# A decay attention and two gated layers on one core: the first layer in two halves for two chunks, fp32 scores on alternating row halves, clustered attention matmuls, early two-operand work on VectorE

## The chip, the cores and the metric

The kernel runs on one core of a Trainium2 chip. The metric is the device time of one execution in microseconds (us). Three runs of the kernel before gave 1046.68, 1047.19 and 1048.68; the median is 1047.19.

The engines in the text: TensorE (PE in the rows; PEld is its weight load), VectorE (DVE), ScalarE (ACT), GpSimd (POOL) and SyncE (SP), which issues the DMA transfers. Each runs its own instructions in the order in which they were issued.

## What is computed

Three stages, each the input of the next. B, H, S, D are 4, 8, 768, 48; the token matrix has 3072 rows of 384.

```python
for t in range(S):                       # attention with a decaying state
    cur = np.einsum('bhd,bhe->bhde', u[None] * kt, vt)
    y[:, :, t] = np.einsum('bhd,bhde->bhe', rt, state + cur)
    state = wt[:, :, :, None] * state + np.einsum('bhd,bhe->bhde', kt, vt)
x = y as (B * S, H * D)
xn = x / np.sqrt(np.mean(x * x, -1) + 1e-6) * rms_g
x = (silu(xn @ w_gate) * (xn @ w_val)) @ w_out     # 384 -> 1536 -> 384, the "first MoE"
g = s * np.maximum(x @ w_in, 0.0) ** 2 + b         # 384 -> 2048, the "second MoE"
out = g @ w_out2                                   # 2048 -> 384
```

The weights come in as 64-bit floats. The result has to be more exact than one matmul of 12-bit parts, so each MoE product is three matmuls: high times high, high times low, low times high.

## The kernel before, in words

**Tiling.** The sequence is cut into six chunks of 128 steps. One chunk of all four batch rows is 512 tokens, the widest matmul. A *pair* (number `jb` = 4 x chunk + batch row, 24 of them) is one batch row's chunk, all eight heads.

**Attention of a pair** (`attention`, L277). VectorE scans the decays forward (L296) and backward (L303); r and k are multiplied with the two results (L257); GpSimd forms the state decay (L309). TensorE makes the scores of four heads that lie on partitions 0 to 47 and of four on 64 to 111 (L332), transposes k (L347), adds up the state's part (L359) and the scores times v (L365), and forms the state's update (L382). ScalarE copies the scores out of PSUM, GpSimd masks them (L337). Then VectorE adds the current step's part, GpSimd computes the row scale (L391, L393), and `attention_x` (L477) transposes the result (L484) into `XH` and `XL`, the high and low parts (L492). From pair 8 on (`FINE = 8`) the scores are made in a finer way: `split_scores` (L423) splits k and r in high and low parts (ScalarE L428 to L432, VectorE or GpSimd L434, L437), multiplies those (L448), adds the pieces, masks them (L455), and splits the masked scores in three bf16 parts (L460, L462); the sums are then six bf16 products (L370).

**First MoE.** A step is one `f` of twelve (128 of the 1536 inner columns): gate and value products (L560), SwiGLU on ScalarE and VectorE, a split of the result in high (`hh`) and low (`hl`) parts, and three output products (L545 to L547) that add up in PSUM banks 2 to 4 over the twelve steps. Per step that is 27 matmuls. At a chunk's end `store` copies the banks out and SP writes them to a scratch tensor `x2d`. Chunk 0 does its first four steps in two token halves of 256 (`HALF = 4`).

**Weights** (`weights`, L497). For each `f` SP loads two blocks of 64-bit words; VectorE builds the 32-bit pattern in three passes (L524, L528, L530) of 768 and of 384 elements, ScalarE takes the high part (L534), VectorE or GpSimd the low part (L536, three per `f`). All 36 tiles of the first MoE stay in SBUF; during chunk 5 the second MoE's tiles overwrite them.

**Second MoE.** Per chunk `x2_in` loads the stored result, splits it, and 16 steps of 18 matmuls follow. Beside them VectorE checks the range of all decays and weights (L656, L673 to L681).

**Order.** Nothing is ordered by hand. Every operation is given to a planner (`Plan`, L96) with a due time, a cost per engine that can do it, and what it reads and writes. It runs through the list in its own time; when an engine comes free, the ready operation with the least due time goes next, and that order is issued. Where an operation names VectorE and GpSimd, the planner picks the one that is free. The due times come from the constants at L44 and the sums over chunks (`dur`, `beg`).

Of the kernel before, what the change touches and what calls it, by code (L numbers as in the profile page):

```python
# [33 lines left out]
G = 16  # L34
# [61 lines left out]
class Plan:  # L96
    """Operations with the engines that can run them, what they read and what they write.

    Each engine runs its operations in the order in which they are issued, so they are issued
    in the order in which they come to be ready: of those that are ready when an engine comes  # L100
    free, the one with the least `when` goes first."""

    PASS = 0.2
# [5 lines left out]
    def add(self, when, engines, fn, reads=(), writes=()):  # L109
# [8 lines left out]
        self.ops.append((when, engines, fn))  # L118
        self.deps.append(deps)

    def issue(self):
# [7 lines left out]
        free = dict.fromkeys(ready, 0.0)  # L129
        done = [False] * n  # L130
# [3 lines left out]
        while events:  # L134
# [8 lines left out]
            for e, queue in ready.items():  # L143
                while queue and free[e] <= now:
# [5 lines left out]
                    cost, late = self.ops[i][1][e]  # L150
                    free[e] = now + cost
                    heapq.heappush(events, (free[e], 0, i))
                    for k in users[i]:
                        left[k] -= 1
                        start = max(now + cost + late, getattr(self, "t%d" % k, 0.0))
                        setattr(self, "t%d" % k, start)
                        if not left[k]:
                            heapq.heappush(events, (start, -1, k))
# [13 lines left out]
def act(n):  # L172
    return 0.20 + 0.55e-3 * n


def gps(n):
    return 0.15 + 2.1e-3 * n


def mm(n, k=1):  # L180
    return k * (0.003 + n / 2400.0)
# [3 lines left out]
def body(ctx: ExitStack, tc: tile.TileContext, rkw, nat, w1, w2, cst, out):  # L185
# [15 lines left out]
    RAW, PAT, SKR, SA = [None] * 2, [None] * 2, [None] * 2, [None] * 2  # L201
# [27 lines left out]
    x2d = [dr.tile([KD, 128, NB], F32, name=f"x2d{c}") for c in range(NC)]  # L229
# [25 lines left out]
    def tt(when, engines, n, dst, a, b, f, reads, writes):  # L255
        cost = {"dve": vec2(n), "pool": gps(n)}
        op(when, {e: cost[e] for e in engines}, lambda e: E[e].tensor_tensor(dst, a, b, f), reads, writes)  # L257
# [19 lines left out]
    def attention(jb, t, quick):  # L277
        q, b = jb % 2, jb % B
        ke, re, ne = QUICK[jb] if quick else (POOL if jb < 2 * B else BOTH, BOTH, BOTH)
# [12 lines left out]
        else:  # L292
# [3 lines left out]
        op(t, {"dve": vec2(HP * WL)}, lambda e: nc.vector.tensor_tensor_scan(  # L296
            ET.rearrange("p h t -> p (h t)"), a[:, 0:HP * WL], ones.rearrange("p h t -> p (h t)"), 0.0,
            ALU.mult, ALU.add), [("w", q), "c"], ["E"])
        op(t, {"pool": 0.06}, lambda e: nc.gpsimd.memset(
            a[:, 0:HP * WL].rearrange("p (h t) -> p h t", h=HP)[:, :, G + 1:C:G], 0.0), ["E"], [("w", q)])  # L300
        op(t, {"dve": 0.27}, lambda e: nc.vector.reciprocal(
            g.rearrange("p (h t) -> p h t", h=HP)[:, :, G - 1:C:G], ET[:, :, G:WL:G]), ["E"], [("g", q)])
        op(t, {"dve": vec2(HP * WL)}, lambda e: nc.vector.tensor_tensor_scan(  # L303
# [4 lines left out]
        if not last:  # L308
            op(t, {"pool": 0.16}, lambda e: nc.gpsimd.tensor_tensor(  # L309
# [8 lines left out]
            AC[q].rearrange("p h o -> p (h o)"), n[0], AX.X, ALU.add), nk, [("ac", q)])  # L318
        tt(td, BOTH, DM, AV[q], v, AC[q].to_broadcast([128, H, D]), ALU.mult, [("ac", q), ("v", q)], [("av", q)])

        A = []
        fine = jb >= FINE
        if fine:
            A = split_scores(t, q, r, k)
            split_v(td, v, n, q)
        for p in range(0 if fine else 2):
            i, s = bank(jb), ring("a", (0, 1, 2))
            sc = PS[i].rearrange("p (h t) -> p h t", h=HP)

            def scores(e, p=p, sc=sc):  # L330
                for h in range(HP):
                    nc.tensor.matmul(sc[:, h, :], k[64 * p:64 * p + D, h, :], r[64 * p:64 * p + D, h, :],  # L332
                                     start=True, stop=True)

            op(t, {"pe": 0.88}, scores, [("k", q), ("r", q)], [("ps", i)])
            cp(t, HP * C, AT[s], sc, [("ps", i)], [("a", s)])
            op(t, {"pool": 0.59}, lambda e, s=s: nc.gpsimd.affine_select(  # L337
                out=AT[s], in_=AT[s], compare_op=ALU.is_gt, fill=0.0, base=0, pattern=[[0, HP], [1, C]],
                channel_multiplier=-1), (), [("a", s)])
            A.append(s)  # L340
        if not last:
# [3 lines left out]
            def turn_k(e, kp=kp):  # L345
# [569 lines left out]
```

## Time and profile before

| | us |
|---|---|
| median of three runs | 1047.19 |
| profiled execution, first to last instruction | 1042.2 |
| TensorE busy | 996.5 (96%) |
| VectorE busy | 745.1 (71%) |
| ScalarE busy | 466.5 (45%) |
| GpSimd busy | 387.8 (37%) |

The profile is of one execution; its own device time is not listed, so its span stands beside the median of the runs, 5.0 us below it. Matmul ends are modelled, so the length of a run of matmuls is read from start to next start. In the page's second part each digit is the busy share of a fortieth of the span (26.06 us) in tenths, and PEclk is the granted clock of TensorE in tenths of 2.4 GHz.

### The profile page before, as it was taken

The numbers are of one execution on the slowest core, as the hardware profiler recorded it, in microseconds if no ns is written. First come the engines' busy times: TensorE is split into PE (matmuls) and PEld (weight loads), VectorE is DVE, ScalarE is ACT, GpSimd is POOL, SyncE is SP. The second block draws the span as 40 slices with busy tenths as digits, with TensorE's granted clock in tenths as the row PEclk, the third lists the DMA queues.
The fourth block names the chain that finished last, engine by engine and source line by source line (L and its number), as shares of the span: only waits on it lengthen the run. The fifth ranks groups of instructions, "written<-read, shape, count | busy, mean of one in ns | idle before, by whom it ended". The sixth has DMA issues, their size and how long they took to land. (4 is left out here: it accounts for less than half of the span.)

```text
span 1042.2 us, 14486 instructions
## 1 busy us (share of the span) xinstructions
PE 996.5 (96%) x5438; PEld 828.6 (80%) x5438; DVE 745.1 (71%) x1115; ACT 466.5 (45%) x899; POOL 387.8 (37%) x389
## 2 busy tenths in 40 slices
PE   8787889999999999999999998999999999999997
PEld 7777778788888888888887776888888888888886
DVE  7999997776776787778669999999973343433333
ACT  2343436655656566665543334334343343433332
POOL 4898556555566556765534553000000000000000
PEclk6598989999999999999999999999999999999999
DMA  8445541212222121112257645757530000000001
GB/s 248 147 157 156 186 144 41 87 50 61 72 66 65 50 90 50 50 49 71 73 145 244 197 157 203 240 199 274 210 112 11 0 31 1 31 1 1 31 1 34
DMA packets 44046, 105.16 MB, mean 101 GB/s; under 512 B 3904, under 2 KB 18752, under 8 KB 43968
## 3 DMA queue, kind: packets, MB, share of 16 engines
q1 hardware_dynamic: 43968, 104.16, 31.1%
q8 instruction: 44, 0.72, 0.3%
q14 instruction: 34, 0.28, 0.1%
HBM read 94.70 MB, written 9.44 MB: 100 GB/s over the span
## 5 line engine op out<-in xcount | busy, mean ns | idle before, releaser
L560 PE MATMUL b<-xh,w 128*128 128x512 f32 (+1 forms) x1494 | 489.8, 389 | 6.6 <-DVE sg L257 2.4
L560 PEld LDWEIGHTS b<-xh,w 128*128 128x128 f32 x1494 | 282.1, 191 | 63.2 <-DVE sg L257 4.1
L560 PE MATMUL b<-xl,w 128*128 128x512 f32 (+1 forms) x747 | 288.2, 386 | 0.0
L546 PE MATMUL b<-hl,w 128*128 128x512 f32 (+1 forms) x519 | 201.8, 389 | 8.2 <-POOL hl L257 7.8
L545 PE MATMUL b<-hh,w 128*128 128x512 f32 (+1 forms) x519 | 205.5, 396 | 2.3 <-ACT hh L260 2.3
L547 PE MATMUL b<-hh,w 128*128 128x512 f32 (+1 forms) x519 | 200.4, 386 | 0.0
L260 ACT ACTIVATE sg<-b 128x512 f32<-128x512 f32 (+1 forms) x173 | 100.7, 582 | 184.4 <-PE b L560 181.1
L560 PEld LDWEIGHTS b<-xl,w 128*128 128x128 f32 x747 | 142.7, 191 | 25.8 <-DVE xl L492 0.2
L626 DVE SCALAR_TENSOR_TENSOR sg<-sg,cs,b 128x512 f32<-128x512 f32 (+1 forms) x97 | 71.8, 741 | 109.4 <-ACT sg L260 109.3
L546 PEld LDWEIGHTS b<-hl,w 128*128 128x128 f32 x519 | 98.4, 190 | 30.3 <-POOL hl L257 11.8
L545 PEld LDWEIGHTS b<-hh,w 128*128 128x128 f32 x519 | 98.4, 190 | 20.3 <-ACT hh L260 2.9
L547 PEld LDWEIGHTS b<-hh,w 128*128 128x128 f32 x519 | 98.2, 189 | 19.1
L629 DVE SCALAR_TENSOR_TENSOR hl<-sg,cs,hh 128x512 fp32r<-128x512 f32 (+1 forms) x97 | 72.2, 744 | 51.1 <-ACT hh L260 51.1
L260 ACT ACTIVATE hh<-sg,cs 128x512 fp32r<-128x512 f32 (+1 forms) x97 | 69.8, 720 | 82.1 <-DVE sg L626 75.6
L257 POOL TENSOR_TENSOR hl<-sg,hh 128x512 fp32r<-128x512 f32 (+1 forms) x52 | 76.7, 1474 | 72.8 <-ACT hh L260 69.1
L260 ACT ACTIVATE hh<-sg 128x512 fp32r<-128x512 f32 (+1 forms) x76 | 46.0, 605 | 67.3 <-DVE sg L257 66.6
L257 DVE TENSOR_TENSOR sg<-b,sg 128x512 f32<-128x512 f32 (+1 forms) x76 | 49.6, 652 | 27.9 <-PE b L560 27.7
L534 ACT ACTIVATE w<-pat 128x384 fp32r<-128x384 f32 x68 | 33.0, 517 | 72.6 <-DVE pat L530 69.5
L536 POOL TENSOR_TENSOR w<-pat,w 128x384 fp32r<-128x384 f32 x36 | 49.9, 1396 | 38.0 <-ACT w L534 38.0
L260 ACT ACTIVATE a<-b 128x256 f32<-128x256 f32 (+1 forms) x80 | 31.7, 417 | 37.4 <-PE b L448 21.4
L460 ACT ACTIVATE sa<-a 128x512 bf16<-128x512 f32 x64 | 39.2, 629 | 20.0 <-DVE a L462 17.3
L530 DVE SCALAR_TENSOR_TENSOR pat<-raw,pat 128x768 uint32<-128x768 uint32 (+1 forms) x40 | 44.0, 1101 | 0.2
(104 smaller groups left out, 1297.1 us busy)
## 6 DMA issues: line engine op xcount, KB each, us to landing
raw<-in_w SPq DMA_DIRECT2D x56, 768.0 KB, 4.6
in<-in_rkw SPq DMA_DIRECT2D x24, 448.0 KB, 3.7
raw<-in_w SPq DMA_DIRECT2D x24, 384.0 KB, 3.4
n<-in_nat SPq DMA_DIRECT2D x23, 384.0 KB, 3.1
in<-in_rkw SPq DMA_DIRECT2D x24, 226.6 KB, 2.5
a<-in_rkw SPq DMA_DIRECT2D x24, 224.0 KB, 3.3
v<-in_nat SPq DMA_DIRECT2D x24, 192.0 KB, 2.6
x2d<-o SPq DMA_DIRECT2D x18, 256.0 KB, 2.3
```

Source lines behind the costliest of these rows:

```text
L257: op(when, {e: cost[e] for e in engines}, lambda e: E[e].tensor_tensor(dst, a, b, f), reads, writes)
L260: op(when, {"act": act(n)}, lambda e: nc.scalar.activation(dst, src, func, **kw), reads, writes)
L460: op(t, {"act": act(N)}, lambda e, s=s, x=x, p=p: nc.scalar.activation(SA[p][:, x], AT[s], AF.Copy), [("a", s)], [("sa", p, x)])
L530: op(t, {"dve": vec2(N)}, lambda e, word=word, pat=pat: nc.vector.scalar_tensor_tensor(pat(), word(0), 29, pat(), ALU.logical_shift_right, ...
L534: op(t, {"act": act(DM)}, lambda e, c=c, s=s, pat=pat: nc.scalar.activation(W[s][:, 0], pat(c).bitcast(F32), AF.Copy), [("pat", pi)], [("w ...
L536: op(t, {"dve": vec2(DM), "pool": gps(DM)}, lambda e, c=c, s=s, pat=pat: E[e].tensor_tensor(W[s][:, 1], pat(c).bitcast(F32), W[s][:, 0].bi ...
L545: nc.tensor.matmul(dst, wt[:, 0, cols], xh, start=first, stop=False, skip_group_check=True)
L546: nc.tensor.matmul(dst, wt[:, 0, cols], xl, start=False, stop=False, skip_group_check=True)
L547: nc.tensor.matmul(dst, wt[:, 1, cols], xh, start=False, stop=last, skip_group_check=True)
L560: nc.tensor.matmul(dst, W[s][:, w, kk * 128:(kk + 1) * 128], xx[x][:, kk, sl], start=first and j == kk == 0, stop=last and kk == KD - 1 an ...
L626: op(t, {"dve": vec2(n)}, lambda e: nc.vector.scalar_tensor_tensor(sg, sg, s_col, p, ALU.mult, ALU.mult), [("ps", i)], [("sg", q)])
L629: op(t, {"dve": vec2(n)}, lambda e: nc.vector.scalar_tensor_tensor(hl, sg, b_col, hh.bitcast(F32), ALU.add, ALU.subtract), [("sg", q), ("h ...
```

## The change

1. **Two halves.** The first MoE's order was: all 12 steps for chunk 0, then for chunk 1, and so on. Now it is steps 0 to 5 for chunk 0, steps 0 to 5 for chunk 1, steps 6 to 11 for chunk 0, steps 6 to 11 for chunk 1, then all 12 for each later chunk. The first half's output sums of the two chunks go to scratch tensors of their own, and `x2_in` loads both and adds them. Chunk 1 does its first six steps in token halves too.
2. **fp32 scores for all pairs, alternating.** The split scores are gone. All pairs multiply k and r directly in fp32, and the matmuls of the two partition halves alternate, into two PSUM banks. The three-part bf16 sums remain, from pair 12 on (`FINE, EARLY = 12, 12`).
3. **Three clusters.** Scores of both halves and the transposes of k are one planner operation; sums of both halves and the state's update are another; the transposes of the result are the third.
4. **Early two-operand work on VectorE.** For pairs 2 to 11 the products of r, k and the current step's part name VectorE alone, as do the low parts of the first MoE's weights and of the SwiGLU result.
5. **The planner.** Costs are changed, the delay from one engine to the next is a number per engine, and two-operand work of VectorE and GpSimd in SBUF excludes each other in its time.

The core of the diff:

```diff
-T0, LAG, LEAD = 18.0, 10.0, 26.0
+T0, LAG = 22.0, 10.0
-HALF = 4
+FA, HALF = 6, (4, 6)
+ATT = 30.0, 6.0, 0.0, 18.0, 20.0, 20.0, 20.0, 0.0
-FINE = 8
+FINE, EARLY = 12, 12
...
-    PASS = 0.2
+    PASS = {"pe": 0.20, "pool": 0.10, "act": 0.15, "dve": 0.12, "sp": 2.0}
...
+                    at = now
+                    free[e] = at + self.ops[i][1][e]
+                    if e in ("dve", "pool") and self.ops[i][3]:
+                        at = max(now, port)
+                        port = free[e] = at + self.ops[i][1][e]
...
-        ke, re, ne = QUICK[jb] if quick else (POOL if jb < 2 * B else BOTH, BOTH, BOTH)
+        ke, re, ne = QUICK[jb] if quick else (DVE, DVE, DVE) if jb < EARLY else (BOTH, BOTH, BOTH)
...
+        def scores(e):
+            for h in range(HP):
+                for p in range(2):
+                    nc.tensor.matmul(sc[p][:, h, :], k[64 * p:64 * p + D, h, :], r[64 * p:64 * p + D, h, :],
+                                     start=True, stop=True)
+            if kp is not None:
+                for h in range(HP):
+                    nc.tensor.transpose(kp[:, h, :], k[:, h, :], ident[:RW, :RW])
...
+        reads = [(n, p, x) for n in ("sa", "sv") for p in range(2) for x in range(3)] if fine else [("a", s) for s in A]
+        op(t, {"pe": (1.3 if fine else 1.8) * slow + 0.9 * (jb >= B) + 0.85 * slow * (not last)}, sums,
+           reads + [("r", q), ("v", q), ("st", b)] + ["kt"] * (not last), [("ps", i)] + ([] if last else [("ps", iu)]))
...
-                op(t, {"dve": vec2(DM), "pool": gps(DM)}, lambda e, c=c, s=s, pat=pat: E[e].tensor_tensor(
+                op(t, {"dve": vec2(DM)} if ph == 0 else {"dve": vec2(DM), "pool": gps(DM)}, lambda e, c=c, s=s, pat=pat: E[e].tensor_tensor(
...
-        tt(t, BOTH, n, HL[q][:, 0:n], sg, HH[q][:, 0:n].bitcast(F32), ALU.subtract, [("sg", q), ("hh", q)], [("hl", q)])
+        tt(t, DVE, n, HL[q][:, 0:n], sg, HH[q][:, 0:n].bitcast(F32), ALU.subtract, [("sg", q), ("hh", q)], [("hl", q)])
+    def moe1_out(t, q, c, f, b0, nb, first, last, part):
+        mm_out(t, (2, 3, 4), slots_of(0, f)[2], q, first and b0 == 0, last, b0, nb)
+        if last:
+            dst = x2d[NC + c if c < 2 and part == 0 else c]
+            store(t, (2, 3, 4), dst, ("x2d", c, part), b0, nb)
...
+            if two:
+                tt(t, ("dve",), NB, r[:, kk], r[:, kk], l.bitcast(F32), ALU.add,
+                   [("xl", x, b, kk) for b in parts], keys)
...
+    for c, p in [(c, p) for p in range(2) for c in range(2)] + [(c, None) for c in range(2, NC)]:
+        fs = range(F1) if p is None else range(FA * p, FA + (F1 - FA) * p)
```

Where the order of an engine moves. Names are those of the program: `in` holds a pair's decays, r and k, `st` its state, `a` masked scores, `b_155` to `b_157` PSUM banks of the attention, `w_74` and on the weight tiles (three per `f`), `xh_111` and `xh_112` the inputs of even and odd chunks. Line numbers of the changed kernel differ (L332 is L339 there, L347 L343, L359 L368, L365 L375, L382 L384, L560 L522, L337 L350).

TensorE before, the sums of pair 4 during chunk 0:

```order
L560 MATMUL b_151<-xh_111,w_84 128x256
L359 MATMUL b_155<-st_70,in_123 128x96 x4
L365 MATMUL b_155<-v_125,a_133 128x48 x4
L347 MATMUL b_157<-cs_63,in_123 128x112 x4
L365 MATMUL b_155<-v_125,a_131 128x48 x4
L382 MATMUL b_156<-v_125,kt_130 112x96 x4
L560 MATMUL b_150<-xh_111,w_74 128x256
```

The transposes of k stand between the two sums there; the scores stand some rows ahead, four matmuls of one half and then four of the other.

TensorE in the changed kernel, the end of chunk 0's first half (`w_91` is the last tile of `f` = 5) and the first of the alternating scores of pair 6:

```order
L507 MATMUL b_154<-hh_118,w_91 128x512
L508 MATMUL b_154<-hl_120,w_91 128x512
L509 MATMUL b_154<-hh_118,w_91 128x512
L446 MATMUL b_157<-cs_63,xg_134 128x128 x3
L339 MATMUL b_155<-in_123 128x128
L339 MATMUL b_156<-in_123 128x128
```

Three more such pairs of rows follow, then the transposes of k and chunk 1's first step, and a step later the sums and the state's update of pair 6 in one piece:

```order
L522 MATMUL b_150<-xh_112,w_77 128x256
L368 MATMUL b_155<-st_72,in_123 128x96 x4
L375 MATMUL b_155<-v_125,a_131 128x48 x4
L375 MATMUL b_155<-v_125,a_132 128x48 x4
L384 MATMUL b_156<-v_125,kt_130 112x96 x4
L507 MATMUL b_152<-hh_117,w_76 128x256
```

What moved: chunk 1 begins after six weight tiles where it began after twelve, and a pair's matmuls stand in three places.

GpSimd before, while chunk 0's weights are made:

```order
L337 AFFINE_SELECT a_132<-a_132 128x512
L391 TENSOR_SCALAR rs_143<-rs_143 128x1
L257 TENSOR_TENSOR n_127<-n_127 128x384
L393 TENSOR_TENSOR rs_143<-rs_143,col_64 128x1
L536 TENSOR_TENSOR w_81<-pat_165,w_81 128x384
L337 AFFINE_SELECT a_131<-a_131 128x512
L536 TENSOR_TENSOR w_82<-pat_167,w_82 128x384
L257 TENSOR_TENSOR in_123<-in_123,eb_129 112x512
L257 TENSOR_TENSOR hl_119<-sg_115,hh_117 128x256
```

GpSimd in the changed kernel, the same stretch of the program:

```order
L350 AFFINE_SELECT a_131<-a_131 128x512
L305 MEMSET in_124 112x4x7
L315 TENSOR_TENSOR pm_140<-eb_128,cs_63 112x8
L263 TENSOR_TENSOR st_70<-st_70,pm_139 112x384
L395 TENSOR_SCALAR rs_143<-rs_143 128x1
L397 TENSOR_TENSOR rs_143<-rs_143,col_64 128x1
```

The low parts (`w`, `hl`) and the products on `n` and `in` have left GpSimd's queue for VectorE's; masks, state decays and row scales remain.

## Rows read from the trace of the kernel before

**Rows 1.** The page's second part: busy tenths in 40 slices, and the clock.

```profile
PE   8787889999999999999999998999999999999997
DVE  7999997776776787778669999999973343433333
PEclk6598989999999999999999999999999999999999
```

**Rows 2.** Windows by stage: length, busy us (instructions) by engine, clock, DMA share, GB/s.

```profile
0.00:34.00 34.00, 25.06 (x108) 21.91 (x108) 26.61 (x40) 9.78 (x21) 17.89 (x27) 0.64 0.75 214
34.00:189.00 155.00, 135.95 (x826) 118.12 (x827) 142.57 (x197) 64.67 (x147) 108.35 (x105) 0.88 0.44 139
189.00:284.00 95.00, 94.07 (x641) 77.94 (x641) 69.73 (x102) 57.53 (x118) 56.78 (x63) 1.00 0.20 61
...
562.00:647.00 85.00, 78.03 (x333) 61.53 (x332) 81.30 (x103) 31.94 (x62) 44.72 (x31) 1.00 0.56 185
647.00:1034.00 387.00, 387.00 (x1720) 320.14 (x1719) 220.74 (x368) 139.85 (x220) 0.00 (x0) 1.00 0.23 81
```

**Rows 3.** Timeline of SP's queue: the first stores of chunks 0 and 1.

```profile
188.97 1.74 SPq L252 DMA_DIRECT2D x2d<-o  x2
...
284.09 1.72 SPq L252 DMA_DIRECT2D x2d<-o  x2
```

**Rows 4.** Timeline of TensorE: ends of nine 256-column and nine 512-column products.

```profile
78.02 0.28 PE L545 MATMUL b<-hh,w 128*128 128x256 f32 x1
...
79.10 0.28 PE L560 MATMUL b<-xh,w 128*128 128x256 f32 x1
...
311.46 0.39 PE L560 MATMUL b<-xh,w 128*128 128x512 f32 x1
...
313.51 0.49 PE L484 MATMUL b<-cs,xg 128*128 128x128 f32 x3
```

**Rows 5.** Timeline of TensorE: scores of two pairs; the second row is 124.14 to 124.59 alone.

```profile
65.13 2.03 PE L332 MATMUL b<-in 48*128 48x128 f32 x16
...
123.93 0.83 PE L332 MATMUL b<-in 48*128 48x128 f32 x9
...
123.60 1.71 PE L332 MATMUL b<-in 48*128 48x128 f32 x16
125.24 0.60 PE L347 MATMUL b<-cs,in 112*128 112x112 f32 x4
```

**Rows 6.** Timeline of TensorE: split scores of a later pair, and the end of a cluster.

```profile
270.30 0.88 PE L448 MATMUL b<-skr 112*128 112x256 f32 x6
271.01 0.40 PE L560 MATMUL b<-xh,w 128*128 128x512 f32 x1
...
306.54 0.48 PE L560 MATMUL b<-xh,w 128*128 128x512 f32 x1
306.86 0.40 PE L560 MATMUL b<-xl,w 128*128 128x512 f32 x1
```

**Rows 7.** VectorE by line: two in 40:160, one in 660:1040, two over the span (min/median/max).

```profile
L536 DVE TENSOR_TENSOR w<-pat,w 128x384 fp32r<-128x384 f32 x19 | 18.2, 974 | 0.0
L528 DVE SCALAR_TENSOR_TENSOR pat<-raw,pat 128x768 uint32<-128x768 uint32 x10 | 13.5, 1349 | 0.1
...
L681 DVE SCALAR_TENSOR_TENSOR pat<-pat 128x768 f32<-128x768 f32 x25 | 23.7, 952 | 0.0
...
L536 DVE TENSOR_TENSOR w<-pat,w x32: 525/850/1644, 23.7 to 632.5; 128x384 fp32r<-128x384 f32 x32
...
L296 DVE TENSOR_TENSOR_SCAN eb<-in,ones x24: 1219/1233/2160, 3.8 to 478.3; 112x516 f32<-112x516 f32 x24
```

**Rows 8.** GpSimd by line in 40:160.

```profile
L536 POOL TENSOR_TENSOR w<-pat,w 128x384 fp32r<-128x384 f32 x14 | 21.6, 1546 | 12.4 <-ACT w L534 12.4
```

**Rows 9.** VectorE by line in 562:647, chunk 5.

```profile
L528 DVE SCALAR_TENSOR_TENSOR pat<-raw,pat 128x768 uint32<-128x768 uint32 x14 | 16.3, 1172 | 0.2
L656 DVE TENSOR_REDUCE wr<-a 112x1 f32<-112x512 f32 x22 | 14.6, 674 | 0.1
```

More of the change, by code (lines that the diff above doesn't have):

```diff
@@ L154, in issue @@
                         left[k] -= 1
-                        start = max(now + cost + late, getattr(self, "t%d" % k, 0.0))
-                        setattr(self, "t%d" % k, start)
+                        begin[k] = max(begin[k], free[e] + self.PASS[e])
                         if not left[k]:
-                            heapq.heappush(events, (start, -1, k))
+                            heapq.heappush(events, (begin[k], -1, k))
         assert len(order) == n
@@ L172, in act @@
 def act(n):
-    return 0.20 + 0.55e-3 * n
+    return 0.10 + 0.825e-3 * n
 def gps(n):
-    return 0.15 + 2.1e-3 * n
+    return 0.15 + 2.13e-3 * n
 def mm(n, k=1):
-    return k * (0.003 + n / 2400.0)
+    return k * (0.013 + n / 2400.0)
 @with_exitstack
@@ L228, in body @@
     b_col = cs[:, CB:CB + 1]
-    x2d = [dr.tile([KD, 128, NB], F32, name=f"x2d{c}") for c in range(NC)]
+    x2d = [dr.tile([KD, 128, NB], F32, name=f"x2d{c}") for c in range(NC + 2)]
     plan = Plan()
@@ L256, in tt @@
         cost = {"dve": vec2(n), "pool": gps(n)}
-        op(when, {e: cost[e] for e in engines}, lambda e: E[e].tensor_tensor(dst, a, b, f), reads, writes)
+        port = not any(k[0] == "ps" for k in reads)
+        op(when, {e: cost[e] for e in engines}, lambda e: E[e].tensor_tensor(dst, a, b, f), reads, writes, port)
     def cp(when, n, dst, src, reads, writes, func=AF.Copy, **kw):
@@ L317, in attention @@
         op(td, {"dve": vec2(DM)}, lambda e: nc.vector.tensor_reduce(
-            AC[q].rearrange("p h o -> p (h o)"), n[0], AX.X, ALU.add), nk, [("ac", q)])
-        tt(td, BOTH, DM, AV[q], v, AC[q].to_broadcast([128, H, D]), ALU.mult, [("ac", q), ("v", q)], [("av", q)])
-        A = []
+            AC[q].rearrange("p h o -> p (h o)"), n[0], AX.X, ALU.add), nk, [("ac", q)], False)
+        tt(td, DVE if jb < EARLY else BOTH, DM, AV[q], v, AC[q].to_broadcast([128, H, D]), ALU.mult, [("ac", q), ("v", q)], [("av", q)])
         fine = jb >= FINE
[L323 to L340, printed above, removed]
+        slow = 1.8 if quick else 1.0
+        i2 = [bank(jb), bank(jb)]
+        sc = [PS[i].rearrange("p (h t) -> p h t", h=HP) for i in i2]
+        kp = None
         if not last:
@@ L371, in sums @@
                                              start=False, stop=end and x == 2, skip_group_check=True)
-            reads = [(n, p, x) for n in ("sa", "sv") for x in range(3)] if fine else [("a", A[p]), ("v", q)]
-            op(t, {"pe": (0.65 if fine else 0.88) + (0.87 if p == 0 and jb >= B else 0.0)}, sums,
-               reads + [("r", q)] + [("st", b)] * (p == 0), [("ps", i)])
-        if not last:
-            iu = bank(jb)
-            U = PS[iu][:RW, 0:DM].rearrange("p (h j d) -> p h j d", h=HP, j=2)
-            def state(e):
+            if U is not None:
                 for h in range(HP):
@@ L464, in split_scores @@
                     [("sa", p, x)], [("a", s)] + [("sa", p, 2)] * x)
-            A.append(s)
-        return A
     def split_v(t, v, n, q):
@@ L732, in later @@
         steps.append((t, len(steps), fn, a))
-    dur = [4 * F1 * 27 * mm(C) + 5.8 * (6, 4, 4, 4, 4, 0)[c] for c in range(NC)]
-    beg = [T0 + sum(dur[:c]) for c in range(NC)]
-    T1 = T0 + sum(dur)
+    step = 27 * mm(NB)
+    beg, parts, t = {}, [], T0
+    for c, p in [(c, p) for p in range(2) for c in range(2)] + [(c, None) for c in range(2, NC)]:
+        fs = range(F1) if p is None else range(FA * p, FA + (F1 - FA) * p)
+        beg[c, p or 0] = t
+        parts.append((c, fs))
+        t += len(fs) * step + ATT[len(parts) - 1]
+    T1 = t
     d2 = F2 * 18 * mm(NB)
```

175 lines of the change are left out of this document (77 added, 98 removed).

## The prediction, made before the changed kernel had run

> **What bounds the kernel now.** I read the page first: TensorE is busy nearly throughout, but its clock line stands at 5 to 9 tenths in the first six slices, which are also the ones where the VectorE line stands at 9 [rows 1]. So the start is a stretch of its own. The windows by stage come next [rows 2], with their bounds taken from the issues that store a finished chunk [rows 3]: chunk 0 ends at 189.0, chunk 1 at 284.1, the first MoE, by the same issues, at about 647. In 189 to 284 TensorE is busy 94.07 of 95 us, in 647 to 1034 all 387: there it is the bound, and only fewer or shorter matmuls help. In 34 to 189 VectorE is busy 142.57 of 155, TensorE works 135.95 at a mean clock of 0.88 (its two levels are 1.2 and 2.4 GHz), and in 562 to 647 VectorE has 81.30 of 85 and TensorE 78.03: in these two stretches VectorE sets the pace.
>
> How much TensorE would need comes from its timeline. Nine 512-column products take 313.51 - 311.46 = 2.05 us, so one step of the first MoE (27) takes 6.15 and a chunk of 12 steps 73.8; nine of 256 columns take 79.10 - 78.02 = 1.08, a half step 3.24 [rows 4]. In 34 to 189 these are 73.8 us, and the attention of six pairs (a pair is one batch row's chunk of 128 tokens) at about 6.7 adds 40: 114 of 155. 41 us go to a waiting or half-clocked TensorE, 11 more in 562 to 647 (85 - 73.8). About 52 us are to be had; the rest is TensorE's own work.
>
> **The change, part by part.**
>
> *Two halves.* Twelve steps on chunk 0 need all twelve weight tiles, each prepared by VectorE. Now six tiles serve chunk 0 and then chunk 1, and the other six come later: TensorE has 24 steps to do while VectorE prepares 12 tiles and attends to pairs 0 to 7. Whether that removes the wait is a sum over VectorE. In the new order 110 VectorE instructions stand ahead of the first SwiGLU product of chunk 0's second token half, and 164 more until the last low half of chunk 1's first six steps. At the durations their kinds have where GpSimd is idle (768-element fields 0.95, not 1.35; 384-element low halves 0.53, not 0.97; a scan 1.23 [rows 7]) they are 69 and 94 us, together 163, or 0.595 each against the 142.57/197 = 0.724 of 34 to 189. VectorE loses 34.0 - 26.6 = 7.4 us in the first 34 [rows 2], so it is there at 7.4 + 163 = 170. What TensorE has left then is 12 full steps (73.8) and pairs 8 to 11 (4 x 5.5): 96. Chunks 0 and 1 would be done at 266. TensorE's own sum from the first place is lower: at 7.4 + 69 = 76 it still has 16 half steps, 14 full ones and 8 pairs, 52 + 86 + 44 = 182, to 258. So VectorE stays the bound until about 170. I take 267 in place of 284.1: **-17**. Bounds: 241, if TensorE never waits (34 + 24 x 6.15 + 3 for the 20 half steps + 2 x 4.6 + 8 x 5.5 for the pairs, + 3), and 302, if instructions keep their mean of 0.724 (7.4 + 198 + 96).
>
> Its price: partial sums of chunks 0 and 1 are stored (9 more stores, with 9 copies out of PSUM at 0.4 to 0.7) and added back with two more loads of 768 KB and six VectorE additions of 0.68. The copies run beside the next half's first products, as at every chunk's end now. The stores stand in SP's queue ahead of later weight loads, so a store that waits for its copy holds those; the tiles then loaded are wanted a half later, which covers it. Three of the additions fall into chunk 5 (2 us, counted below), three into the second MoE. Taken at nothing; without cover some 5.
>
> *Two-operand work on VectorE.* In 40 to 160 GpSimd does 44 such instructions, 14 of them low halves at 1.55 us [rows 8]. On VectorE they are 24.8 us at clean durations, and its own excess in that window, 19 x 0.45 for the low halves, 10 x 0.40 for fields and so on, is 28. So VectorE's load hardly moves, while a low half arrives a microsecond earlier. This is already in the 163. What remains on GpSimd (masks, row scales, state decays), some 40 of its 108 us in 34 to 189, still collides; I set that against the 0.08 us by which consecutive instructions overlap, about 20 us over the 274.
>
> *Scores.* Before, a pair's 16 score passes run on one row half and then the other: 2.03 us [rows 5]. At 123.60 both halves happened to be ready together, and the 16 took 125.24 - 123.60 = 1.64; in the 0.45 us from 124.14 nine passes ran or started, where 2.03/16 = 0.127 a pass would let in four or five. So the halves can run side by side, and alternating them all through should give 8 steps of 0.11 plus 0.2 at the ends: 1.1. Bounds 1.1 and 2.03. For pairs 0 to 7 this and fewer clusters save about 1.2 us each, mostly where VectorE sets the pace. For pairs 12 to 23 the split scores go, 8 passes of 0.119 (six of them 271.01 - 270.30 = 0.71 [rows 6]), 0.95: against 1.1 a loss of 0.15.
>
> Here the Trainium skill speaks against the change: the page TensorEngine Tiling (Array Packing), Key Properties, says that a change of tiling mode drains the TensorE, and the new scores put a 64-row stretch into later pairs that had none. No row prices a drain by itself; what a row shows is that the first product after a cluster takes 0.32 in place of 0.23 (306.54 to 306.86 [rows 6]). Two such ends over 12 pairs are 2 us, and they stand in the 1.1.
>
> *Three clusters.* Each return from an fp32 or bf16 cluster to the MoE products costs that 0.09 us. Late pairs had five, now three: 12 x 2 x 0.09 = 2. Together with the 0.15 above (12 x 0.15 = 2) nothing is left in chunks 2 to 4. The wait it adds: sums of both halves and the state now wait for the later mask and for kt, with MoE products queued behind on TensorE; the order places at least one step between scores and sums, so I take nothing.
>
> *Less on VectorE and ScalarE from pair 8 on.* Six ScalarE copies and some eight VectorE or GpSimd operations per pair go with the split scores. Chunks 2 to 4 are TensorE-bound, so this buys 1 us in all. In chunk 5 VectorE's 81.30 holds about 14 us of excess over clean durations (14 tiles' fields, at 1.17 where 0.95 is clean, and their like), which I let go, since the new order gives no low half of the first MoE to GpSimd there. It gains twelve of them at 0.68 and 2 us of additions; the decay checks stay (22 reductions at 0.67 fell into this stretch, and of 48 the new order has 18 ahead of the second MoE's first weight field, before none) [rows 9]. That leaves some 77 beside TensorE's 73.8: 85 becomes 79, **-6**.
>
> *Sum.* 1042.2 - 17 - 1 - 6 = 1018.2 of span. The median of the runs, 1047.19, stands 5.0 above the profiled span, so **1023**.
>
> **The rivals.** (1) *TensorE never waits*: VectorE's overlap is worth more than the remaining collisions, chunks 0 and 1 end at 241 and chunk 5 takes 74.5: 1042.2 - 43 - 1 - 10 + 5 = 993. For it: the sum at 258 without VectorE. Against: the half-clocked stretches of slices 1 to 4 return whenever TensorE waits. (2) *VectorE stays as slow as it is* and now has GpSimd's work too: the mean of 0.724 gives 302 for chunks 0 and 1, +18, with -7 later: **1058, slower**. It decides from 0.685 us an instruction (7.4 + 274 x 0.685 + 96 = 291, +7 against the -7). For it: the number of VectorE instructions rises; against: the same fields take 0.95 where GpSimd is idle. (3) *The halves of the scores do not overlap*, or each change of mode drains for long: 0.9 us more for the 16 pairs in stretches that TensorE bounds, +15: 1038. For: 0.127 a pass is the usual picture; against: the nine. (4) *The gain is eaten*: the stores of partial sums and the coarser clusters cost what the halves bring: about 1047.
>
> **How the numbers follow.** A measurement of this kernel tells about 0.2% (2 us) from no change. Forecast 0.70, rival 1 0.11, rival 3 0.09, rival 2 0.07, rival 4 0.03. The range 997 to 1043 takes in the forecast with its unknown costs and rival 3, and cuts most of 1 and all of 2 and 4. Faster 0.91, same 0.02, slower 0.07.
>
> **What would show it.** Right: the first stores of chunk 1's final sums near 267, low halves and fields on VectorE near 0.53 and 0.95 before that, a row of 16 score passes in about 1.1 us, 75 to 81 us for chunk 5, 387 for the second MoE unchanged. Wrong in its main step: fields still at 1.2 to 1.35 with GpSimd half empty, or TensorE waiting in the first 170 us as long as now. If TensorE is full from 100 us on, rival 1 holds.

## The result, and the profile after

The changed kernel takes 1013.72 us (median of four runs, 1012.13 to 1014.33); the kernel before took 1047.93 beside it. The ratio is 0.968, its 95% interval 0.9655 to 0.9704. The forecast was 1023 (997 to 1043). The profiled execution took 1012.13, with a span of 1010.4.

The page's second part (busy tenths in 40 slices of 25.26 us; before: [rows 1]):

```profile
PE   6789999999999999999999999999999999999997
DVE  7889999355655555556579889999994443433332
PEclk7689999999999999999999999999999999999998
```

TensorE's clock stands at 9 tenths or more from the fourth slice on, where this came with the seventh. VectorE stands at 7 to 9 tenths until 177 us and then at 3 to 6 up to 505, where it stood at 6 to 8. Stage ends are read as before, from the first store of a finished chunk, here in the timeline of SP's queue for chunks 1, 4 and 5:

```profile
264.44 0.34 SPq L257 DMA_DIRECT2D x2d<-o  x1
...
538.66 0.34 SPq L257 DMA_DIRECT2D x2d<-o  x1
...
612.10 0.33 SPq L257 DMA_DIRECT2D x2d<-o  x1
```

The same for chunks 4 and 5 in the kernel before:

```profile
562.58 0.34 SPq L252 DMA_DIRECT2D x2d<-o  x1
...
646.66 0.81 SPq L252 DMA_DIRECT2D x2d<-o  x2
```

| us | before | forecast | after |
|---|---|---|---|
| chunks 0 and 1 end | 284.1 | 267 | 264.4 |
| chunks 2 to 4 | 278.5 | 277.5 | 274.2 |
| chunk 5 | 84.1 | 78.1 | 73.4 |
| from there to the span's end | 395.5 | 395.5 | 398.3 |
| span | 1042.2 | 1018.2 | 1010.4 |

Windows of these stages (columns as in [rows 2]):

```profile
0.00:34.00 34.00, 23.01 (x121) 20.40 (x121) 27.30 (x45) 9.35 (x20) 13.69 (x24) 0.67 0.75 221
34.00:170.00 136.00, 123.72 (x938) 114.81 (x937) 125.51 (x243) 59.38 (x146) 31.38 (x45) 0.94 0.51 161
170.00:264.40 94.40, 94.40 (x541) 79.81 (x540) 50.41 (x81) 32.94 (x69) 27.21 (x38) 1.00 0.23 66
264.40:538.70 274.30, 274.30 (x1950) 230.38 (x1949) 165.67 (x256) 122.71 (x247) 119.03 (x136) 1.00 0.30 87
538.70:612.10 73.40, 73.40 (x325) 60.79 (x325) 62.98 (x82) 30.16 (x57) 27.88 (x24) 1.00 0.54 177
612.10:1003.60 391.50, 390.15 (x1733) 321.89 (x1732) 240.33 (x398) 143.25 (x229) 4.35 (x3) 1.00 0.27 89
```

From 170 us to 612 TensorE shows no idle time. In chunk 5 it has its 73.4 us of own work and nothing else, and VectorE has 10 us to spare there.

VectorE by line in 40:160 (before: [rows 7], [rows 8]):

```profile
L498 DVE TENSOR_TENSOR w<-pat,w 128x384 fp32r<-128x384 f32 x30 | 16.2, 560 | 0.6 <-ACT w L496 0.6
L492 DVE SCALAR_TENSOR_TENSOR pat<-raw,pat 128x768 uint32<-128x768 uint32 x11 | 10.4, 948 | 0.0
L302 DVE TENSOR_TENSOR_SCAN eb<-in,ones 112x516 f32<-112x516 f32 x6 | 7.4, 1225 | 0.0
```

VectorE's timeline at the two places of the forecast's sum, the 110th and the 274th instruction (the second row merges two low halves, at 161.48 and 161.95):

```profile
72.11 0.95 DVE L492 SCALAR_TENSOR_TENSOR pat<-raw,pat 128x768 uint32<-128x768 uint32 x1
...
161.48 1.02 DVE L498 TENSOR_TENSOR w<-pat,w 128x384 fp32r<-128x384 f32 x2
```

A low half takes 0.560 where it took 0.974 (and 1.546 on GpSimd), a field 0.948 for 1.349, a scan 1.225 for 1.673 in the same window. VectorE works off 243 instructions in 136 us of this stretch, where it took 155 for 197 [rows 2].

### The profile page after: what moved, and what is told of

Its sections match the earlier page's. It is cut to its first block, busy times and chain, and to the rows that moved or that the text cites. A ratio compares the mean times of both kernels' runs of the same rounds, so it can differ in the third digit from the quotient of the medians.

```text
span 1010.4 us, 14457 instructions
## 1 busy us (share of the span) xinstructions
PE 979.3 (97%) x5600; PEld 828.2 (82%) x5600; DVE 672.2 (67%) x1101; ACT 398.5 (39%) x767; POOL 223.6 (22%) x268
## 4 chain that ended last, share of the span: by engine, by line
PE 81%; DVE 4%; DMA 3%; ACT 1%; issue 1%; SPq 0%; ACTq 0%; DVEq 0%
PE b L522 43%; PE b L508 10%; PE b L507 10%; PE b L509 10%; DMA raw<-in_w 2%; PE b L339 2%; PE b L368 1%; PE b L380 1%; PE b L384 1%; PE b L375 1%; PE b L343 1%; PE b L446 1%; DVE hl L592 0%; DVE pat L652 0%; DVE ws L647 0%
## 5 line engine op out<-in xcount | busy, mean ns | idle before, releaser
L522 PE MATMUL b<-xh,w 128*128 128x512 f32 (+1 forms) x1566 | 488.7, 377 | 3.1 <-ACT w L496 1.3
L522 PEld LDWEIGHTS b<-xh,w 128*128 128x128 f32 x1566 | 290.6, 191 | 56.0 <-ACT w L496 1.8
L522 PE MATMUL b<-xl,w 128*128 128x512 f32 (+1 forms) x783 | 292.8, 374 | 0.2 <-DVE xl L454 0.2
L522 PEld LDWEIGHTS b<-xl,w 128*128 128x128 f32 x783 | 149.1, 191 | 25.3 <-DVE xl L454 0.4
L508 PEld LDWEIGHTS b<-hl,w 128*128 128x128 f32 x537 | 101.2, 189 | 22.9 <-DVE hl L263 2.8
L507 PEld LDWEIGHTS b<-hh,w 128*128 128x128 f32 x537 | 101.2, 188 | 19.3 <-ACT in L553 0.9
L509 PEld LDWEIGHTS b<-hh,w 128*128 128x128 f32 x537 | 101.0, 188 | 18.4
L350 POOL TENSOR_SCALAR_AFFINE_SELECT a<-a 128x512 f32<-128x512 f32 x48 | 45.0, 956 | 92.6 <-ACT a L266 92.5
L263 DVE TENSOR_TENSOR hl<-sg,hh 128x512 fp32r<-128x512 f32 (+1 forms) x82 | 53.1, 647 | 13.9 <-ACT hh L266 13.4
L498 POOL TENSOR_TENSOR w<-pat,w 128x384 fp32r<-128x384 f32 x28 | 34.2, 1238 | 67.3 <-ACT w L496 64.4
L266 ACT ACTIVATE a<-b 128x512 f32<-128x512 f32 x48 | 26.6, 594 | 43.8 <-PE b L339 42.5
L339 PE MATMUL b<-in 48*128 48x128 f32 x384 | 31.1, 306 | 9.4 <-DVE in L263 6.6
```

The costliest lines, as they stand in the source:

```text
L266: op(when, {"act": act(n)}, lambda e: nc.scalar.activation(dst, src, func, **kw), reads, writes)
L339: nc.tensor.matmul(sc[p][:, h, :], k[64 * p:64 * p + D, h, :], r[64 * p:64 * p + D, h, :], start=True, stop=True)
L350: op(t, {"pool": 0.60}, lambda e, s=A[p]: nc.gpsimd.affine_select(out=AT[s], in_=AT[s], compare_op=ALU.is_gt, fill=0.0, base=0, pattern=[[ ...
L498: op(t, {"dve": vec2(DM)} if ph == 0 else {"dve": vec2(DM), "pool": gps(DM)}, lambda e, c=c, s=s, pat=pat: E[e].tensor_tensor(W[s][:, 1], ...
L507: nc.tensor.matmul(dst, wt[:, 0, cols], xh, start=first, stop=False, skip_group_check=True)
L508: nc.tensor.matmul(dst, wt[:, 0, cols], xl, start=False, stop=False, skip_group_check=True)
```

## The experiments

Stages are those of each run's profiled execution, read from the stores. All runs stand beside the kernel before on the same chip (1046.74 to 1047.93 in the four sets), so medians compare to some 2 us. Every edit makes the planner write a new order: one_delay and first_five, which change neither what is computed nor which engines may do it, end chunks 0 and 1 by 4 and 10 us later. A shift of that size at the start shows a cause only where rows name it. The edit is against the changed kernel unless it says otherwise; times and stages in us, the ratio is to the kernel before.

| run | median | ratio, 95% interval | chunks 0, 1 | 2 to 4 | 5 | rest |
|---|---|---|---|---|---|---|
| the change | 1013.72 | 0.968, 0.9655 to 0.9704 | 264.4 | 274.2 | 73.4 | 398.3 |
| one_pass | 1028.25 | 0.9817, 0.9784 to 0.985 | 277.6 | 272.7 | 75.3 | 401.2 |
| lows_shared | 1035.45 | 0.9878, 0.984 to 0.9916 | 285.8 | 273.7 | 76.8 | 399.0 |
| pairs_shared | 1020.33 | 0.9734, 0.9704 to 0.9763 | 271.3 | 274.2 | 73.5 | 398.0 |
| no_alternate | 1027.68 | 0.9816, 0.9783 to 0.9848 | 273.5 | 280.4 | 73.4 | 398.6 |
| six_clusters | 1016.46 | 0.9716, 0.9682 to 0.975 | 267.3 | 274.6 | 73.5 | 397.4 |
| old_rules | 1026.65 | 0.9779, 0.9747 to 0.9811 | 270.5 | 276.9 | 81.9 | 396.4 |
| no_exclusion | 1037.04 | 0.9903, 0.987 to 0.9937 | 271.7 | 273.5 | 83.9 | 399.9 |
| one_delay | 1018.61 | 0.9731, 0.9698 to 0.9764 | 268.3 | 273.0 | 76.6 | 398.3 |
| before_vector | 1041.6 | 0.9949, 0.9928 to 0.997 | 283.3 | 278.6 | 77.7 | 395.9 |
| before_checks | 1039.89 | 0.992, 0.9889 to 0.9952 | 284.8 | 277.1 | 81.5 | 395.2 |
| first_five | 1022.1 | 0.9767, 0.9733 to 0.9801 | 274.3 | 272.7 | 73.4 | 398.1 |
| first_eight | 1020.81 | 0.975, 0.9717 to 0.9783 | 262.8 | 283.1 | 73.4 | 397.3 |

**one_pass.** The core of the edit (due times follow the old formulas):

```diff
-    for c, p in [(c, p) for p in range(2) for c in range(2)] + [(c, None) for c in range(2, NC)]:
-        fs = range(F1) if p is None else range(FA * p, FA + (F1 - FA) * p)
+    for c in range(NC):
+        fs = range(F1)
```

> The changed kernel with the first MoE's twelve steps in one pass per chunk again (chunk 0, then chunk 1), all else as in the change. Theory A (the two halves carry the gain of the start): chunk 1's last sums are stored at 278 to 285 us in place of 264, the time is 1027 to 1034. Rival B (VectorE freed of GpSimd's collisions does it alone): stored by 270, time under 1020.

Theory A, by its time and just short of its 278: 277.6. TensorE's waits for VectorE in 34:300 (us in total, times, longest; in the change these are 0.3, 2.0 and none):

```profile
PE b L522 <- DVE sg L263: 5.4, 2, 4.6
PE b L508 <- DVE hl L263: 4.3, 3, 1.7
PE b L339 <- DVE in L263: 2.0, 1, 2.0
```

Even with fast VectorE instructions, twelve tiles for one chunk keep TensorE waiting for VectorE. The halves are worth 13 us at the start, and 14.5 in all.

**lows_shared.**

```diff
-                op(t, {"dve": vec2(DM)} if ph == 0 else {"dve": vec2(DM), "pool": gps(DM)}, lambda e, c=c, s=s, pat=pat: E[e].tensor_tensor(
+                op(t, {"dve": vec2(DM), "pool": gps(DM)}, lambda e, c=c, s=s, pat=pat: E[e].tensor_tensor(
-        tt(t, DVE, n, HL[q][:, 0:n], sg, HH[q][:, 0:n].bitcast(F32), ALU.subtract, [("sg", q), ("hh", q)], [("hl", q)])
+        tt(t, BOTH, n, HL[q][:, 0:n], sg, HH[q][:, 0:n].bitcast(F32), ALU.subtract, [("sg", q), ("hh", q)], [("hl", q)])
```

> The changed kernel with the low halves (of the first MoE's weights and of the SwiGLU result) on VectorE or GpSimd again. Theory A (a low half on GpSimd comes late and slows VectorE): chunks 0 and 1 end 5 to 10 us later, chunk 5 takes 79 to 84 in place of 73.4, with TensorE waiting for a low half on GpSimd; time 1024 to 1034. Rival B (chunk 5 is shorter because 14 decay checks of 0.67 have left it, the low halves have nothing to do with it): chunk 5 stays under 76, time 1010 to 1019.

At the start theory A, and at least twice as dear as it said: 21 us, all that chunks 0 and 1 had won. Waits in 34:170:

```profile
PE b L522 <- POOL w L498: 4.5, 2, 2.6
PE b L508 <- POOL hl L263: 3.1, 3, 1.6
```

The window of this run, and VectorE's fields in 40:160:

```profile
34.00:170.00 136.00, 113.80 (x775) 103.67 (x775) 101.14 (x174) 50.84 (x126) 70.22 (x71) 0.82 0.46 144
...
L490 DVE SCALAR_TENSOR_TENSOR pat<-raw,pat 128x768 uint32<-128x768 uint32 x9 | 8.9, 989 | 0.0
L492 DVE SCALAR_TENSOR_TENSOR pat<-raw,pat 128x768 uint32<-128x768 uint32 x8 | 7.6, 947 | 0.0
```

The two waits make 7.6 us. TensorE is idle 22.2 us there, against 12.3 in the change, and its clock is 0.82, against 0.94; how the rest of the 21 us divides was not measured. Of theory A the lateness is shown, the slower VectorE hardly: its fields take 0.947 and 0.989, and it is busy 101 of 136 us. Chunk 5 takes 3.4 us more, so neither theory holds there: TensorE waits 0.8 in it, and 2.0 are nine products that stand behind chunk 4's store here and ahead of it in the change.

**pairs_shared.**

```diff
-FINE, EARLY = 12, 12
+FINE, EARLY = 12, 0
```

> The changed kernel with the r, k, n and av products of pairs 2 to 11 on VectorE or GpSimd again, the low halves still on VectorE. Theory A (what GpSimd takes over costs VectorE as much in slower fields and scans): 768-element fields above 1.05 us before 160 us, chunks 0 and 1 end at 266 to 275, time 1015 to 1025. Rival B (GpSimd really relieves VectorE): they end by 262, time 1006 to 1012.

Theory A by place and time (271.3 and 1020.33), though the fields rose less than it said; 7 us is a shift that a new order alone can make. VectorE by line in 40:160:

```profile
L492 DVE SCALAR_TENSOR_TENSOR pat<-raw,pat 128x768 uint32<-128x768 uint32 x10 | 10.3, 1030 | 0.0
L302 DVE TENSOR_TENSOR_SCAN eb<-in,ones 112x516 f32<-112x516 f32 x5 | 7.8, 1560 | 0.0
```

**no_alternate.**

```diff
-            for h in range(HP):
-                for p in range(2):
+            for p in range(2):
+                for h in range(HP):
                     nc.tensor.matmul(sc[p][:, h, :], k[64 * p:64 * p + D, h, :], r[64 * p:64 * p + D, h, :],
```

> The changed kernel with the eight score products of one partition half and then those of the other, in the same cluster. Theory A (alternating lets the two halves run side by side): 16 passes take 1.8 to 2.03 us in place of 1.09; 14 pairs lie where TensorE is the bound, 14 x 0.7 to 0.94, time 1023 to 1028. Rival B (16 passes in one cluster are fast whatever their order): 16 passes within 0.2 us of 1.09, time 1011 to 1016.

The timeline of TensorE, pair 14, of the change, with the matmuls on both sides:

```profile
297.59 0.39 PE L522 MATMUL b<-xh,w 128*128 128x512 f32 x1
297.91 1.16 PE L339 MATMUL b<-in 48*128 48x128 f32 x16
299.00 0.60 PE L343 MATMUL b<-cs,in 112*128 112x112 f32 x4
299.38 0.48 PE L522 MATMUL b<-xh,w 128*128 128x512 f32 x1
299.70 0.40 PE L522 MATMUL b<-xl,w 128*128 128x512 f32 x1
```

The same pair in this run:

```profile
307.57 1.71 PE L339 MATMUL b<-in 48*128 48x128 f32 x16
309.21 0.60 PE L343 MATMUL b<-cs,in 112*128 112x112 f32 x4
```

From the first score to the transposes it is 299.00 - 297.91 = 1.09, and 309.21 - 307.57 = 1.64 without alternating. Theory A in kind; its 1.8 to 2.03 was too long, yet its time holds, because all pairs pay: 11 pairs in chunks 2 to 4 make 11 x 0.55 = 6.1, and the stage grew by 6.1. The start grew by 9, since its first pairs run at the lower clock (3.02 for 2.01). The starts of the single passes show how: in the change two passes, one of each half, start 0.007 us apart, and the next two some 0.11 later. Here four passes of the first half start alone before the second half runs beside it.

**six_clusters** (transposes of k, the sum of each half and the state's update as operations of their own again):

```diff
-        op(t, {"pe": (1.1 + 0.45 * (not last)) * slow}, scores, [("k", q), ("r", q), "cs"],
-           [("ps", i) for i in i2] + ([] if last else [("ps", i)]))
+        op(t, {"pe": 1.1 * slow}, scores, [("k", q), ("r", q), "cs"], [("ps", i) for i in i2])
+        if not last:
+            op(t, {"pe": 0.45 * slow}, turn_k, [("k", q), "cs"], [("ps", i)])
...
+        for p in range(2):
+            def sums(e, p=p):
...
+        def state(e):
```

> The changed kernel with the transposes of k, the two sums and the state's update as planner operations of their own again (six clusters per pair), scores alternating in one. Theory A (a cluster costs 0.09 us of return and nothing else; the waits of chunks 2 to 4 came from the split scores, whose PSUM banks VectorE had to empty): 3 x 0.09 x 14 pairs, time 1015 to 1019, no wait of the transposes for VectorE. Rival B (small clusters wait for banks and copies by themselves): waits of 0.4 us or more ahead of the transposes or the state's update in each pair, time 1021 to 1027.

Theory A by its time. No transpose waits in chunks 2 to 4; clusters there rise from 34 to 56 (counted where a product of the MoE is followed by another matmul), and the products' mean spacing from 0.2320 to 0.2345, 2.4 us over 978 of them. With every return at 0.085 to 0.09, 22 more would be 1.9. The stage as a whole grows by 0.4 alone, because the sums of one pair that lie in it in the change lie outside it here. The other stages move by less than 3.

What six clusters do not show was in the kernel before: TensorE's timeline around the transposes of k of one pair there:

```profile
202.24 0.40 PE L547 MATMUL b<-hh,w 128*128 128x512 f32 x1
203.20 0.60 PE L347 MATMUL b<-cs,in 112*128 112x112 f32 x4 [0.57 <-DVE a L257]
```

And TensorE's waits there in 189:562 (us in total, times, longest):

```profile
PE b L347 <- DVE a L257: 2.5, 6, 0.6
PE b L546 <- POOL hl L257: 0.7, 2, 0.4
```

The split scores filled PSUM banks that VectorE had to empty (`a`), and the transposes, which needed one of them, held TensorE. No run keeps the split scores in the changed kernel, so this rests on these waits and on their absence here.

**old_rules, no_exclusion, one_delay.** The planner's two rules, both and each by itself:

```diff
-    PASS = {"pe": 0.20, "pool": 0.10, "act": 0.15, "dve": 0.12, "sp": 2.0}
+    PASS = {"pe": 0.20, "pool": 0.20, "act": 0.20, "dve": 0.20, "sp": 2.0}
...
-                    if e in ("dve", "pool") and self.ops[i][3]:
+                    if False:
```

> The changed kernel with the planner's rules of before: one delay of 0.2 for all engines, and no exclusion between VectorE and GpSimd in its time (costs as in the change). Theory A (the rules only shuffle the order of one engine's work by a place or two): chunks 0 and 1 end at 262 to 268, time 1011 to 1017. Rival B (without the exclusion the plan is too early for VectorE, and its order no longer suits TensorE): chunks 0 and 1 end past 270, time 1020 or more.

> The changed kernel with the planner's exclusion between VectorE and GpSimd alone taken out (its delays per engine stay). Theory A (the exclusion is the rule that counts: with it the plan sees VectorE as full in chunk 5 and leaves the decay checks and fields for later): some 20 of the 0.67 us reductions in chunk 5 in place of 8, chunk 5 at 80 to 83 us, time 1021 to 1027. Rival B (the delays per engine count): 8 to 12 reductions, chunk 5 under 76, time 1012 to 1018.

> The changed kernel with one delay of 0.2 us for every engine in the planner (the exclusion stays). Theory A (the exclusion counts): chunk 5 under 75 us, time 1012 to 1018. Rival B (the delays count): chunk 5 at 80 or more, time 1021 to 1027.

The rules are worth 13 us (old_rules, theory B), over half of it in chunk 5. VectorE by line in chunk 5 of old_rules (547.4 to 629.3):

```profile
L490 DVE SCALAR_TENSOR_TENSOR pat<-raw,pat 128x768 uint32<-128x768 uint32 x14 | 15.4, 1097 | 0.1
L627 DVE TENSOR_REDUCE wr<-a 112x1 f32<-112x512 f32 x20 | 13.3, 673 | 0.0
```

TensorE's waits in the same stretch:

```profile
PE b L522 <- DVE sg L263: 4.8, 6, 1.6
PE b L508 <- DVE hl L263: 1.2, 3, 0.6
```

And VectorE by line in chunk 5 of the change (538.5 to 612):

```profile
L490 DVE SCALAR_TENSOR_TENSOR pat<-raw,pat 128x768 uint32<-128x768 uint32 x13 | 14.7, 1134 | 0.0
L263 DVE TENSOR_TENSOR hl<-sg,hh 128x512 fp32r<-128x512 f32 x12 | 8.4, 702 | 0.5 <-ACT hh L266 0.5
L627 DVE TENSOR_REDUCE wr<-a 112x1 f32<-112x512 f32 x8 | 5.4, 677 | 0.0
```

With both rules 8 reductions of the decay checks lie in chunk 5, with neither 20, and without the exclusion alone 21; that stage takes 73.4, 81.9 and 83.9. A plan that holds VectorE for free while GpSimd works lets checks in, and VectorE then keeps TensorE waiting. The checks are not all of it: of the 17.5 us that VectorE is busier in old_rules' chunk 5 (80.50 for 62.98), twelve reductions are 7.9 and six low halves of the second MoE 5.2. One delay for all engines costs 5 us by itself, near theory A; 2.0 of the 3.2 us in its chunk 5 are again nine products on the other side of chunk 4's store. no_exclusion has theory A's reductions, but its median is above the 1021 to 1027: it costs 23 us, more than both rules together, so the two do not add. Its runs spread from 1030.75 (the profiled one) to 1039.2, so some 6 of the 23 are in no profile, and that is open.

**before_vector, before_checks**, both made from the kernel before. The first names VectorE alone where the change's fourth part does:

```diff
-        ke, re, ne = QUICK[jb] if quick else (POOL if jb < 2 * B else BOTH, BOTH, BOTH)
+        ke, re, ne = QUICK[jb] if quick else (DVE, DVE, DVE) if jb < 12 else (BOTH, BOTH, BOTH)
...
-        tt(t, BOTH, n, HL[q][:, 0:n], sg, HH[q][:, 0:n].bitcast(F32), ALU.subtract, [("sg", q), ("hh", q)], [("hl", q)])
+        tt(t, DVE, n, HL[q][:, 0:n], sg, HH[q][:, 0:n].bitcast(F32), ALU.subtract, [("sg", q), ("hh", q)], [("hl", q)])
```

(and so for `av` and the weights' low parts). The second lets a check's load wait for chunk 5's last sum:

```diff
-        dma(t, w, rkw[jb, :, 0:HP * WL].rearrange("p (h t) -> p h t", h=HP)[:, :, 1:], RW * HP * C * 4, (), [("a", s)])
+        dma(t, w, rkw[jb, :, 0:HP * WL].rearrange("p (h t) -> p h t", h=HP)[:, :, 1:], RW * HP * C * 4, [(("x2d", NC - 1), 2, 0)], [("a", s)])
```

> The kernel before with the fourth part of the change alone: r, k, n and av products of pairs 2 to 11, the low halves of the first MoE's weights and of the SwiGLU result on VectorE only. Theory A (VectorE's load hardly moves, low halves arrive earlier): chunks 0 and 1 end at 276 to 284 us (before 284), chunk 5 takes 78 to 81 (before 84.3), time 1034 to 1043. Rival B (without the two halves VectorE becomes the bound): chunks 0 and 1 end past 288, time 1049 or more.

> The kernel before with the loads of the decay checks held until the last sum of chunk 5 is stored, so that none of the 22 reductions of 0.67 us lies in chunk 5. Theory A (these reductions delay what TensorE waits for in chunk 5): chunk 5 takes 75 to 79 in place of 84.3, the second MoE up to 3 longer, time 1038 to 1043. Rival B (low halves on GpSimd are the wait): chunk 5 stays at 82 or more, time 1045 to 1050.

before_vector is theory A by its time; its ten runs spread from 1037.28 (the profiled one) to 1046.04. The start hardly moves (283.3), where it meets other waits: a mask on GpSimd holds the sums for 8.5 us in 34:300. Chunk 5 falls by 6.4 to 77.7 although 26 reductions lie in it:

```profile
L656 DVE TENSOR_REDUCE wr<-a 112x1 f32<-112x512 f32 x26 | 17.2, 676 | 1.2 <-DMA a<-in_rkw 1.2
```

before_checks has theory A's time but not its place: with no reduction in it, chunk 5 still takes 81.5, and the largest wait there is that for the low half on GpSimd:

```profile
PE b L546 <- POOL hl L257: 2.4, 4, 0.9
```

So two causes are seen in chunk 5's 10.6 us: low halves on GpSimd (6.4 alone) and checks (2.6 alone). Neither alone brings the 73.4. With the low halves moved and checks kept VectorE is nearly full (75.17 of 77.70 in before_vector, 80.50 of 81.90 in old_rules); but old_rules, with fewer checks, takes 4 us more, so the number of checks does not set the stage by itself.

**first_five, first_eight.**

```diff
-FA, HALF = 6, (4, 6)
+FA, HALF = 5, (4, 5)
```

In first_eight the new line is `FA, HALF = 8, (4, 6)`.

> The changed kernel with five steps in the first half and seven in the second (FA, HALF = 5, (4, 5)). Theory A (after 150 us TensorE never waits, and before that VectorE is the bound whatever the split): chunks 0 and 1 end at 261 to 268, time 1010 to 1018. Rival B (fewer tiles ahead of chunk 1 let TensorE start it earlier and wait less before 150): they end by 259, time 1004 to 1009.

> The changed kernel with eight steps in the first half and four in the second (FA, HALF = 8, (4, 6)). Theory A (chunk 1 can only start when eight tiles are there, which brings back part of the wait of the single pass): chunks 0 and 1 end at 267 to 273, time 1016 to 1023. Rival B (the size of the first half does not matter): 262 to 266, time 1011 to 1016.

Neither gains. Five ends the start 10 us later, against both theories; eight has theory B's place, 1.6 earlier than the change, and theory A's time, because chunks 2 to 4 give back 9. The due times (`ATT`) were left as they are for six, and no run tells the split apart from them: that is open. No kernel tried is faster than the change.

## Why the prediction was right

**Start: the place right, in part by luck.** The forecast put VectorE's last low half of the first six steps of chunk 1 at 170 and chunk 1's end at 267: measured 162.5 and 264.4. Its parts: 110 instructions were to take 69 us and 164 more 94; their recorded durations add up to 69.0 and 96.8, so the durations without collisions were the right ones. The step that was off is the last choice, remaining collisions set against the overlap of consecutive instructions (20 us): the overlap was there (19.6), hardly any collision was, and VectorE sat idle for 16.3 us up to there in place of 7.4, which hid part of the miss: it was 8 us earlier. From there TensorE needed 101.9 in place of 96, so two misses cancel. Nor did VectorE stay the bound until 170. From the end of the 110th instruction to chunk 1's end TensorE was nearly full:

```profile
73.06:264.40 191.34, 186.99 (x1276) 166.02 (x1274) 141.77 (x258) 77.03 (x176) 52.24 (x71) 1.00 0.37 115
```

It waits 4.4 us there, the last time at 147, and its own work takes 187 us where the forecast's second sum, the one that ended at 258, had 182. With these waits that sum, TensorE's own, gives the end that was measured. Rival 1's 241 fails all the same: between 34 and 73 us TensorE waits 7.9 us, and its clock is 0.78 in 34:60. Of the 12.3 us that it waits in 34:170, nearly half are for ScalarE:

```profile
PE b L446 <- ACT xg L266: 5.8, 3, 3.0
```

lows_shared and one_pass show that both parts are needed: each taken away alone loses 13 to 21 of the 20 us, so shares cannot be added up. The Trainium skill's page SBUF — State Buffer, section Who interferes with whom, says that a VectorE instruction with two SBUF inputs contends with a GpSimd instruction that reads SBUF and that the later one blocks. The 768-element fields (0.948, 1.030 in pairs_shared, 1.349 before) agree. One by one, those in 40:160 that no GpSimd instruction overlaps in time take 0.94 to 0.95 on average in all of these runs; the overlapped ones, both kinds of field, take 1.43 on average before, 1.18 in pairs_shared, 0.99 in lows_shared, and 0.95 in the change, where mostly masks, row scales and state decays remain on GpSimd. An overlap alone does not slow a field.

**Scores: right.** 16 passes in 1.09 for the 1.1 forecast, in eight steps of 0.11 as it said. The reason was half right: the 1.64 at 123.60 was taken as a chance overlap of halves, but no_alternate gives 1.64 for any two halves back to back in one cluster. The 2.03 of [rows 5], from which the 0.127 a pass came, runs to a modelled end; from first to last start that row is 1.76. Rival 3 falls. Of what the change of mode costs, the rows now show more: entering the scores costs 0.32 in place of 0.23, as the return does (297.59 to 297.91, 299.38 to 299.70), while entering transposes or sums costs nothing (0.23 on average in chunks 2 to 4). This entry stands ahead of the first score, so the 1.1 did not hold it. The Trainium skill's page TensorEngine Tiling (Array Packing), Key Properties, also says that different tiles can work in parallel, and 1.09 against 1.64 agrees.

**Chunks 2 to 4: -4.3 for -1.** The term of clusters (2 us) missed a wait: in [rows 6]'s kind of pair the transposes waited for banks that VectorE empties, and the state's update for ScalarE's copy of kt. Spacing ahead of the transposes was 0.52 on average and ahead of the update 0.33, where 0.23 is free of a wait (means of 270:540); for the 7 pairs that have them in these chunks this is 7 x 0.29 + 7 x 0.10 = 2.7. Waits for low halves on GpSimd were 0.7 more.

**Chunk 5: -10.6 for -6.** The forecast let the checks stay in it, 22 reductions of 0.67. The planner's rules had moved them, 8 are left, and 13 sets of fields in place of 14: VectorE is busy 62.98 of the 77 forecast. The rules were priced by their order alone, and old_rules shows 8.5 us in this stage from them. Rival 1's figure for it, 74.5, was the better one. 0.9 of the 10.6 only moved: four products that stood ahead of the store now stand behind it.

**Second MoE: +3 for 0.** Those four products are 0.9 of it. 11 of the checks' 48 reductions now lie there, none before: in 700:750 VectorE is busy 49.72 of 50 us, where it was 40.71 in the like stretch before (735:785). TensorE waits in 612:1003:

```profile
PE b L507 <- ACT in L553: 0.7, 1, 0.7
PE b L508 <- DVE hl L592: 0.6, 2, 0.4
```

The first stands at the very end and is no matter of checks. Some 0.9 of the 3.1 up to the last matmul is not traced.

**From span to time.** 5.0 was added, the median against the profiled span. In the change the same difference is 3.3 (1013.72 against 1010.4). The profiled execution of the kernel before was a short one of its kind: its runs spread from 1043.81 to 1051.45 in these sets. That is 1.7 of the forecast's 9.3 us too many; 7.8 lie in the span (the forecast dropped 0.2 in rounding). Rivals 2 and 4 fall; partial sums cost no visible wait in chunk 5. One argument against rival 1, that half-clocked stretches return whenever TensorE waits, was too strong: in 562 to 647 before it waits 7 us at a clock of 1.00 [rows 2].

## What to carry to other kernels

Where preparing weights on a second engine holds the first, use each prepared tile for two batches of work before the next is prepared; count the instructions of the preparing engine up to a place in the program, at durations from where its neighbour is quiet, and add up the other engine's own work from the same place: the later of the two sums sets the end. An operation moved away from a contended engine is judged by what the other instructions of the receiving engine then take, not by its own duration on either. In a list scheduler, leave no low-priority work in what it thinks is a gap: check which work it let in, stage by stage.

## What was not expected of the hardware

Passes of 48 rows on alternating halves of the array started every 0.068 us on average (1.09/16), in twos 0.007 apart; half after half every 0.1025 (1.64/16). At the lower clock, in the first 50 us, the same 16 took 2.01 and 3.02. Going from 128-row products to 48-row passes cost 0.09 us, about as much as the way back from scores, transposes or sums; the split scores, 112 rows with 256 columns, cost 0.01 both ways (0.24 for 0.23).
